# Talking-heads attention and squared-ReLU feed-forward on one core: one load of values at another step, and the score bursts of a batch's last block at other gathers

## Chip, cores and metric

The kernel runs on one core of one Trainium2 chip. The metric is device time in microseconds (us). The kernel before takes 598.79 us, the median of three runs (598.04 to 600.64).

## What is computed

Eight batches of attention with 12 heads, 448 positions and a head dimension of 64. The scores of the heads are mixed by a 12 x 12 matrix before the softmax, the probabilities by a second one behind it. The result, 3584 rows of 768, goes through a feed-forward layer with a squared ReLU and 2048 hidden units.

```python
scores = scale * np.matmul(q, k.transpose(0, 1, 3, 2))
scores = np.einsum('bhij,hg->bgij', scores, w_pre)
scores = scores - np.max(scores, axis=-1, keepdims=True)
attn = np.exp(scores)
attn = attn / (np.sum(attn, axis=-1, keepdims=True) + 1e-09)
attn = np.einsum('bhij,hg->bgij', attn, w_post)
attn_out = np.matmul(attn, v)
...
x = np.ascontiguousarray(attn_out.transpose(0, 2, 1, 3)).reshape(B * S, H * D)
h = np.maximum(x @ w_in, 0.0)
return (h * h @ w_out).astype(np.float32)
```

Inputs and output are float32; inside, the operands of matmuls are bfloat16.

## The kernel before

**Tiles and steps.** The queries of a batch are worked on ten at a time: ten queries by 12 heads are the 120 partitions of one tile. A batch has 45 such tiles (`NT`), and the eight batches make 360 steps, numbered through (`i`): batch 0 has steps 0 to 44, batch 1 has 45 to 89. One step does `mix` of tile i (matmul with the mixing matrix into `m_ps`, L420; exp on ScalarE, L424; every second tile the reciprocal of the sums on VectorE, L431, and the scaled mixing matrix `pn` on GpSimd, L434) and `unmix` of tile i - 4 (matmuls into `at_ps`, L449 and L453; copy into `at` by VectorE, L455). In the first 20 tiles of batch 0 scores and mixing are one set of matmuls (L406).

**Scores and gathers.** The scores are made for blocks of 128 queries, all heads: a batch from the second on has four blocks, which begin at queries 0, 128, 256 and 384 (`STARTS`); the last has 64 queries. A block's scores lie in a tile `S` with queries on the partitions, of which there are two in turn, so a block overwrites the one before the last. `score_burst` makes them for some pairs of heads: six matmuls (L359; twelve small ones, L365, for a last block) into six of the eight PSUM banks, and six copies into `S`, three by ScalarE (L369) and three by VectorE (L371). `gather` reshapes: one DMA on SP's queue (L388; two in a last block, L391) takes a tile's ten queries of all heads out of `S` into a tile `G` with 120 partitions, of which there are twelve. Gathers run ten steps ahead of their use (`AHEAD`). `FIRST` holds the tile at which the gathers of each block begin: 0, 13, 26 and 39. The scores of the following block are started at the gathers that `BURSTS` lists, counted from the block's first as 0: for the four blocks at [5, 8], [5, 8], [6] and [0, 3]. So the scores of the next batch's first block are made at the gathers of tiles 39 and 42, which stand at steps 29 and 32 of each batch (74 and 77 for batch 1). Tile 38 is the last to read the block that their `S` tile held before.

**Loads.** GpSimd issues all loads from DRAM, each at the top of a given step (`at_load`), in one queue (q0), with a cast to bfloat16. A batch's values come in three loads (`load_v`): the first rows of each group for the lower 64 partitions (L252), those for the upper 64 (L252), and the seventh row for the lower partitions (L248, the third load). There are two tiles of values, for even and odd batches. The values are first used in the matmuls of `av_unit` (L227 for the first three slots, L234 for the last two), three steps after a third of the tiles has been unmixed; for batch 1 this is step 66. `V1_AT` holds the steps at which the three loads of batch 1 are issued; `KQ_AT`, `W1_AT` and `W2_AT` those of keys and queries of batches 1 and 2 and of the weights. Later batches load their values at steps 34, 37 and 40 of the batch before.

**Feed-forward.** The hidden units of a batch (`ffn1_unit`, matmuls L278, relu on ScalarE L284, square on GpSimd or VectorE L289) and the output (`ffn2_unit`, matmuls L322, copy by VectorE L331, stores on SP L303) fill the steps of the next batch, spread by `fill`.

**Order.** The order on TensorE and GpSimd is the program's own (`manual_schedule`); VectorE's and ScalarE's instructions are put in order by a scheduler; SP's gathers and stores stand in one queue.

Of the kernel before, what the change touches and what calls it, by code (L numbers as in the profile page):

```python
# [30 lines left out]
STARTS = {0: (FQ, S - 128)}  # L31
FIRST = {0: (FUSED, 32)}
BURSTS = {0: ([4, 8], [5, 8])}
for _b in range(1, B):
    STARTS[_b], FIRST[_b], BURSTS[_b] = (0, 128, 256, 384), (0, 13, 26, 39), ([5, 8], [5, 8], [6], [0, 3])
GATHERS_AT = 2
HALF = H // 2
TT = 15
# [5 lines left out]
KQ_AT = {1: (4, 7, 10, 12), 2: (49, 51, 53, 55)}  # L44
W1_AT = (-1, 1, 3, 14, 16, 18)
W2_AT = (27, 29, 31, 33, 36, 39, 42, 45)
V1_AT = (46, 48, 56)
EARLY = ((21, 0, 0, 2), (29, 0, 2, 4), (38, 1, 0, 4), (52, 2, 0, 4))
FFN2_AT = 60
MAIN = 3 * 128  # L50
# [3 lines left out]
def kernel(  # L54
# [422 lines left out]
    with tc.manual_schedule(engines={PE, POOL}):  # L477
# [12 lines left out]
        def at_load(i, f, *args):  # L490
            loads.setdefault(i, []).append(lambda: f(*args))

        at_load(6, load_v, 0, 2)
        for x in range(3):
            at_load(V1_AT[x], load_v, 1, x)
        for x in range(4):
# [108 lines left out]
```

## Time and profile before

| | us |
|---|---|
| median of three runs | 598.79 |
| the profiled execution | 596.65 |
| its span, first to last instruction | 594.9 |
| VectorE busy in it | 401.7 |
| ScalarE busy | 380.7 |
| GpSimd busy | 355.5 |
| SP's stretch of 14 gather issues of batch 1's last block, from 120.86 us on | 11.68 |

The profile is that of one execution. PE is TensorE's matmuls, PEld its weight loads, DVE is VectorE, ACT ScalarE, POOL GpSimd, SP the queue of gathers and stores. A row of instructions in order of time reads: start, length, engine, line, operation, output<-input, shape, count, and in brackets the engine's idle time before it with what ended it. A row of waits reads: who waited, for whom, total us, times, longest. The clock row has a digit for each of 40 equal slices of the span, in tenths of full speed.

### The profile page before, as it was taken

The page shows a single profiled execution, that of the slowest core. Times are in us where ns is not written, and L with a number is a line of the kernel's source. Part 1 is how long each engine was busy: PE and PEld are TensorE (multiplying, and loading weights), DVE is VectorE, ACT ScalarE, POOL GpSimd, SP SyncE. Part 2 cuts the span into 40 slices and gives each one's busy share as a digit, 9 for nine tenths or more (in the row PEclk, how much of TensorE's full clock was granted, in tenths as well). Part 3 has the DMA queues.
Part 4 walks back from the last instruction along what each step waited for, and adds up shares of the span by engine and source line. Part 5 has one row for each costly group of instructions (what it writes and reads, how often), then busy time and mean ns, then how long its engine had stood idle before and what let it go on. Part 6 is the DMA issues. An engine that isn't in the chain of part 4 may idle for free.

```text
span 594.9 us, 18505 instructions
## 1 busy us (share of the span) xinstructions
PE 568.8 (96%) x6735; PEld 364.4 (61%) x6735; DVE 401.7 (68%) x995; ACT 380.7 (64%) x1114; POOL 355.5 (60%) x812
## 2 busy tenths in 40 slices
PE   4999999798999999999999999999999999999997
PEld 2577776464665665666665665655665666666554
DVE  7758759486877668777877668867777667655011
ACT  3747977476877548775777548775678548762410
POOL 6467896264579436784479436783486535772740
PEclk9999999898999999999999999999999999999999
DMA  9998999389557955688557955687643865432113
GB/s 129 156 192 171 184 196 178 74 130 200 135 106 121 167 118 99 122 132 160 116 81 130 173 122 102 116 134 144 125 81 65 126 136 110 87 50 54 28 26 81
DMA packets 85579, 72.28 MB, mean 122 GB/s; under 512 B 18768, under 2 KB 80496, under 8 KB 85488
## 3 DMA queue, kind: packets, MB, share of 16 engines
q1 hardware_dynamic: 49354, 47.30, 36.1%
q0 software_dynamic: 35552, 23.60, 30.2%
q8 instruction: 53, 0.87, 0.6%
q10 hardware_dynamic: 582, 0.21, 0.1%
q14 instruction: 38, 0.31, 0.1%
HBM read 47.28 MB, written 11.01 MB: 98 GB/s over the span
## 4 chain that ended last, share of the span: by engine, by line
PE 86%; DMA 7%; ACT 2%; POOL 2%; issue 1%; DVE 1%; SPq 0%; ACTq 0%; POOLq 0%; DVEq 0%
PE o_ps L322 23%; PE h_ps L278 23%; PE m_ps L420 10%; PE at_ps L449 9%; PE ot_ps L227 5%; PE s_ps L359 4%; PE m_ps L406 4%; DMA G<-S 3%; DMA v<-in_v_dram 2%; PE tr_ps L212 2%; PE ot_ps L234 2%; PE at_ps L453 2%; ACT e L424 1%; PE s_ps L365 1%; ACT S L369 1%
## 5 line engine op out<-in xcount | busy, mean ns | idle before, releaser
L455 DVE CAST at<-at_ps 128x480 bf16<-128x480 f32 (+1 forms) x360 | 206.7, 592 | 70.8 <-PE at_ps L453 53.7
L424 ACT ACTIVATE e<-m_ps 120x448 bf16<-120x448 f32 x360 | 196.2, 550 | 89.9 <-PE m_ps L420 49.0
L434 POOL TENSOR_SCALAR pn<-post,rc 120x120 bf16<-120x120 bf16 (+1 forms) x340 | 122.7, 371 | 175.8 <-DVE rc L431 111.7
L278 PE MATMUL h_ps<-xt,w 128*128 128x448 bf16 (+2 forms) x960 | 169.0, 315 | 2.3 <-ACT S L369 1.6
L322 PE MATMUL o_ps<-w,h 128*128 128x384 bf16 x768 | 140.5, 329 | 0.4
L420 PE MATMUL m_ps<-G,pre 120*120 120x448 bf16 (+1 forms) x340 | 122.0, 359 | 1.0 <-ACT S L369 0.5
L278 PEld LDWEIGHTS <-w 128*128 128x128 bf16 x960 | 84.3, 98 | 59.0 <-issue 8.7
L449 PE MATMUL at_ps<-pn,e 120*128 120x120 bf16 x1080 | 116.2, 216 | 4.0 <-ACT S L369 1.8
L289 POOL TENSOR_TENSOR h<-hr 128x384 bf16<-128x384 f32 (+1 forms) x144 | 105.7, 736 | 21.7 <-ACT hr L284 19.7
L449 PEld LDWEIGHTS <-e 120*128 120x128 bf16 x1080 | 85.8, 98 | 47.5 <-ACT S L369 4.5
L284 ACT ACTIVATE hr<-h_ps 128x448 f32<-128x448 f32 (+2 forms) x160 | 75.7, 478 | 46.8 <-PE h_ps L278 36.3
L322 PEld LDWEIGHTS <-h 128*128 128x128 bf16 x768 | 73.8, 99 | 47.2 <-issue 5.1
L369 ACT CAST S<-s_ps 128x448 bf16<-128x448 f32 x177 | 82.2, 551 | 14.4 <-PE s_ps L359 9.3
L371 DVE CAST S<-s_ps 128x448 bf16<-128x448 f32 x141 | 80.2, 614 | 3.8 <-DMA G<-S 3.5
L424 ACT ACTIVATION_READ_ACCUMULATOR e<-m_ps 120x1 f32 x360 | 75.5, 210 | 0.0
L331 DVE COPY osb<-o_ps 128x384 f32<-128x384 f32 x54 | 30.1, 557 | 58.7 <-PE o_ps L322 58.6
L431 DVE RECIPROCAL rc<-sm 120x1 f32<-120x1 f32 (+1 forms) x192 | 31.1, 162 | 43.7 <-ACT e L424 30.5
L420 PEld LDWEIGHTS <-pre 120*120 120x120 bf16 (+1 forms) x340 | 45.2, 133 | 20.8 <-issue 12.0
L240 ACT CAST xt<-ot_ps 128x450 bf16<-128x450 f32 (+1 forms) x48 | 25.4, 532 | 29.8 <-PE ot_ps L234 29.5
L437 POOL TENSOR_TENSOR en<-e,rc 120x128 bf16<-120x128 bf16 (+1 forms) x112 | 42.6, 380 | 0.0
L227 PE MATMUL ot_ps<-at,v 128*64 128x150 bf16 x864 | 42.2, 231 | 0.0
L359 PE MATMUL s_ps<-kT,qT 64*128 64x448 bf16 x276 | 39.6, 355 | 1.4 <-ACT hr L284 0.5
(62 smaller groups left out, 476.5 us busy)
## 6 DMA issues: line engine op xcount, KB each, us to landing
G<-S SPq DMA_DIRECT2D x276, 105.0 KB
out_dram<-osb SPq DMA_DIRECT2D x54, 192.0 KB
kst<-in_k_dram POOLq DMA_DIRECT2D x14, 336.0 KB, 5.8
qst<-in_q_dram POOLq DMA_DIRECT2D x14, 336.0 KB, 6.2
G<-S SPq DMA_DIRECT2D x70, 52.5 KB
v<-in_v_dram POOLq DMA_DIRECT2D x8, 384.0 KB, 9.0
w<-in_moe_w_in_dram POOLq DMA_DIRECT2D x6, 512.0 KB, 10.8
w<-in_moe_w_out_dram POOLq DMA_DIRECT2D x8, 384.0 KB, 8.2
```

The source lines that it names most:

```text
L227: nc.tensor.matmul(ps[64 * hh:64 * hh + 64, TQ * y:TQ * y + TQ], lhsT=vts[b % 2][:, g, r, :], rhs=at[:, r, g, :, :].rearrange("p t i -> p ...
L278: nc.tensor.matmul(ps[:, 0:n], lhsT=w1[ft // 8][:, c2, ft % 8 * 128:ft % 8 * 128 + 128], rhs=xts[b][:, c2, n0:n1], start=(c2 == 0), stop=( ...
L284: nc.scalar.activation(out=hr[:, 0:n], in_=ps[:, 0:n], func=ACT.Relu)
L289: eng.tensor_tensor(out=dst[:, x - o:y - o], in0=hr[:, x - n0:y - n0], in1=hr[:, x - n0:y - n0], op=ALU.mult)
L322: nc.tensor.matmul(ps[:, 0:384], lhsT=lhsT, rhs=w2[ft // 4][:, ft % 4, nt * 384:(nt + 1) * 384], start=(ft == 0), stop=(ft == FT - 1))
L369: nc.scalar.copy(out=sb[:, h, :], in_=ps[:, 0:S])
L371: nc.vector.tensor_copy(out=sb[:, h, :], in_=ps[:, 0:S])
L420: nc.tensor.matmul(ps[0:n, 0:S], lhsT=m[0:n, 0:n], rhs=Gs.pop(s)[0:n, :], start=True, stop=True)
L424: nc.scalar.activation(out=e[0:n, x, :], in_=ps[0:n, 0:S], func=ACT.Exp, scale=SCALE, accum_out=sm[0:n, x:x + 1])
L434: nc.gpsimd.tensor_scalar(out=esb[(b, t - z)][1][0:rows, :], in0=(post_gi if fused else post)[0:rows, :], scalar1=rc[0:rows, z:z + 1], sca ...
L449: nc.tensor.matmul(ps[:, RG * r:RG * r + RG], lhsT=e[0:n, tl % 2, P * r:P * r + P], rhs=pn[0:n, :], start=True, stop=True)
L455: nc.vector.tensor_copy(out=ats[(b, third)][:, 0:k, :, tl, :], in_=ps[:, 0:k * RG].rearrange("p (r g i) -> p r g i", r=k, i=IQ))
```

## The change

Two constants. The third load of batch 1's values is issued at the top of step 24, in place of step 56. The scores for a next batch's first block are started at the gathers 2 and 4 of a last block (its third and fifth, tiles 41 and 43), in place of 0 and 3; in step numbers these stand at 31 and 33 of a batch in place of 29 and 32. This holds for the six batches 1 to 6.

```diff
-    ..., BURSTS[_b] = (0, 128, 256, 384), (0, 13, 26, 39), ([5, 8], [5, 8], [6], [0, 3])
+    ..., BURSTS[_b] = (0, 128, 256, 384), (0, 13, 26, 39), ([5, 8], [5, 8], [6], [2, 4])
...
-V1_AT = (46, 48, 56)
+V1_AT = (46, 48, 24)
```

In the program's order TensorE's burst matmuls move, six at a time; the six copies behind each move with them on ScalarE and VectorE; GpSimd's issue of the load moves; SP's order is the same.

More of the change, by code (lines that the diff above doesn't have):

```diff
@@ L34 @@
 for _b in range(1, B):
-    STARTS[_b], FIRST[_b], BURSTS[_b] = (0, 128, 256, 384), (0, 13, 26, 39), ([5, 8], [5, 8], [6], [0, 3])
+    STARTS[_b], FIRST[_b], BURSTS[_b] = (0, 128, 256, 384), (0, 13, 26, 39), ([5, 8], [5, 8], [6], [2, 4])
 GATHERS_AT = 2
```

## The prediction

> **What bounds the kernel now.** I read the page first (busy shares, granted clock), then the list of waits, then the instructions in order of time around each long wait of TensorE.
>
> ```profile
> PE 568.8 (96%) x6735; PEld 364.4 (61%) x6735; DVE 401.7 (68%) x995; ACT 380.7 (64%) x1114; POOL 355.5 (60%) x812
> PEclk9999999898999999999999999999999999999999
> ...
> q0 software_dynamic: 35552, 23.60, 30.2%
> ```
>
> TensorE is busy for 568.8 of 594.9 us, so all that a change of order can win is in the 26 us left. Two slices of the clock row (about 104 to 119 and 134 to 149 us) stand under full speed; q0 is the queue of POOL's loads. The list of waits says who makes TensorE wait, and who waits for a DMA:
>
> ```profile
> PEld L234 <- DMA v<-in_v_dram: 3.6, 1, 3.6
> DVE S L371 <- DMA G<-S: 3.5, 5, 1.7
> PE ot_ps L234 <- DMA v<-in_v_dram: 3.4, 1, 3.4
> ACT S L369 <- DMA G<-S: 3.3, 2, 1.9
> ```
>
> There is one wait of 3.4 us for a load of values, and there are seven waits of the score copies (L369, L371) for a gather. In order of time, TensorE's matmuls:
>
> ```profile
> 101.98 1.47 PE L322 MATMUL o_ps<-w,h 128*128 128x384 bf16 x8
> ...
> 103.92 0.39 PE L227 MATMUL ot_ps<-at,v 128*64 128x150 bf16 x6
> 107.70 0.26 PE L234 MATMUL ot_ps<-at,v 128*64 128x80 bf16 x4 [3.39 <-DMA v<-in_v_dram]
> ...
> 110.59 2.10 PE L322 MATMUL o_ps<-w,h 128*128 128x384 bf16 x8
> ...
> 139.03 0.38 PE L449 MATMUL at_ps<-pn,e 120*128 120x120 bf16 x3 [1.78 <-ACT S L369]
> ...
> 389.66 1.29 PE L278 MATMUL h_ps<-xt,w 128*128 128x448 bf16 x6 [1.40 <-ACT S L369]
> ```
>
> These three are the only waits of TensorE over 0.9 us after the start. Stretches of time show what the others did in the first wait, and the clock after the first two (length; busy us of PE, PEld, DVE, ACT, POOL; clock; DMA share, GB/s):
>
> ```profile
> 104.00:107.70 3.70, 0.31 (x8) 0.13 (x8) 0.65 (x3) 0.89 (x4) 1.63 (x5) 1.00 0.72 172
> 108.46:111.88 3.42, 3.42 (x43) 2.44 (x37) 0.66 (x1) 1.70 (x4) 0.00 (x0) 0.50 0.00 0
> 139.18:142.60 3.42, 3.37 (x16) 1.85 (x15) 1.75 (x4) 2.16 (x7) 0.84 (x3) 0.50 1.26 233
> ```
>
> In the 3.70 us no engine is busy even for half the time: nothing else was late, and the load alone set the end. Then TensorE ran 3.42 us at half its clock.
>
> **Part one: the third load of batch 1's values from step 56 to step 24.** It removes nothing and adds nothing; one DMA issue of POOL moves forward.
>
> ```profile
> 49.36 0.70 POOL L434 TENSOR_SCALAR pn<-post,rc 120x120 bf16<-120x120 bf16 x2 [2.46 <-PE tr_ps L212]
> ...
> 92.81 0.80 POOL L248 DMA_DIRECT2D v<-in_v_dram  x1
> ```
>
> Issued at 92.81, the data were there when the wait ended, just under 107.70: some 14.8 us. It is the last of seven loads that POOL issues from 79.4 us on, so it arrives last. At step 24 (about 47 us) it has 57 us until the same use, and the earlier copy of this load for batch 0, also in a crowded stretch, took 14.1 us. So:
> - The wait at 107.70 goes: -3.39 us. Bounds -3.39 and 0 (something else late in its place: a rival below).
> - The half clock behind it goes: TensorE is busy for 3.42 of 3.42 us at 0.50, and the same work takes 1.71 at full clock: -1.71. The eight L322 matmuls show it, 2.10 us there (partly at full clock again) and 1.47 before. Bounds -1.71 and 0.
> - The issue takes 0.80 us of POOL at its new place. POOL sits idle for 2.46 us before 49.36, which is where its order puts the load, so 0. Without that cover pn would be 0.8 us late, and TensorE's at_ps (L449) waits for pn: +0.8 at most.
> - Queue q0: the loads issued behind it (eight of w_out, 52.9 to 77.6 us) move back. The load is 96 KB; at the 174 and 163 GB/s of the stretches 46.9-52.9 and 52.9-59.2 us that is 0.6 us. They land 6.3 to 8.7 us after issue, so the last by 86.4 us, and their first use (L322) is at 98.9: 12 us of cover, so 0. Gathers share those engines and could be 0.6 us late; they run ten steps ahead: 0, at most +0.6.
> - At step 56 POOL gains 0.80 us, ahead of an idle time of 2.90 us: 0.
>
> [...]
>
> **Part two: score bursts at the third and fifth gather of a batch's last block.** Six places (batches 1 to 6). The first burst of six matmuls moves two steps later, the second one step; the count of matmuls, copies and gathers is the same, and SP's order too. The first burst writes the S buffer of block two, whose last reader is the gather just before: its copies wait for that gather, keep six of eight PSUM banks, and TensorE stands. Seen at batch 5:
>
> ```profile
> 387.19 0.74 PE L359 MATMUL s_ps<-kT,qT 64*128 64x448 bf16 x6
> ...
> 389.07 1.40 ACT L369 CAST S<-s_ps 128x448 bf16<-128x448 f32 x3 [1.37 <-DMA G<-S]
> ```
>
> Two steps are some 3.3 us (594.9 / 360 = 1.65 each), more than the 1.9 us from the burst to its copies' start, so this wait goes: -1.40. At the other five places the same burst costs TensorE under 0.5 us each. All waits of copies for gathers sum to 6.8 us; 3.6 of these (1.9 and 1.7) belong to the stall at 139.03, which is a burst at the sixth gather of batch 2, not moved. That leaves 3.2 as the most that can be won; I take the row, 1.40.
>
> What it may cost: the bursts stand two steps apart, not three. DVE's three copies end 2.54 us after their burst began:
>
> ```profile
> 325.24 0.74 PE L359 MATMUL s_ps<-kT,qT 64*128 64x448 bf16 x6
> ...
> 326.10 1.68 DVE L371 CAST S<-s_ps 128x448 bf16<-128x448 f32 x3
> ```
>
> Against 3.3 us that leaves 0.8; at the shortest pair seen (122.17 to 125.81, three steps in 3.64, so two in 2.43) it is 0.1 short. Bounds 0 and six times 1.68 = 10.1; nearest are the rows, so +0.3 in all. Behind the second burst, SP's first gather of the next block comes two steps later: 3.3 against 2.54, no wait; if there were one, later gathers and the stores queue behind it, with ten steps (16 us) of cover.
>
> The stall at 139.03 I leave as it is: SP issues its gathers back to back there, and neither part touches that. [...]
>
> **Sum:** -3.39 - 1.71 - 1.40 + 0.3 = -6.2 us. The profiled execution took 596.65 us (span 594.9, 1.75 around it); less 6.2 that is 590.45. It lies 2.1 under the median of the timed runs (598.79; 598.04 to 600.64), and I take the difference from the median: 592.6 us.
>
> **Rivals.**
> 1. The load's wait is replaced by one for gathers. For: in the 3.7 us stall the DMAs moved 172 GB/s, 636 KB, six gathers of 105 KB: a backlog was cleared in the pause. Against: at that rate a gather takes 0.6 us and TensorE uses one per 1.65, with twelve buffers. If 3.39 comes back and the clock stays up: 598.79 - 1.71 - 1.1 = 596.0.
> 2. Part two wins nothing, or its closer bursts eat it: -5.1 with 0 to 2 back: 593.7 to 595.7.
> 3. Slower: with two steps between bursts the second finds its banks held at all six places, and each stall is like that at 139.03: 6 x 1.78 = 10.7, so 598.79 - 6.5 + 10.7 = 603.0. It decides from 1.6 us a place ((6.5 + 3.0) / 6). For: 139.03 shows what six held banks do. Against: there the copies waited for a gather; here for nothing but their engines.
> [...]
> 5. The stall at 139.03 goes as well, being fed by a queue that now starts from another state: 592.6 - 1.78 - 1.71 = 589.1.
> 6. The load at step 24 does not arrive earlier: nothing supports this, as its order on POOL is fixed; under 0.01.
>
> **Numbers.** Forecast 0.50; rivals 1: 0.12, 2: 0.14, 3: 0.06, 4: 0.08, 5: 0.10. A measurement of this kernel tells from no change what exceeds 0.5% (3.0 us). Faster than 595.8: forecast, 4, 5 and nearly all of 2: 0.80. Same: rival 1 and what is left of 2: 0.14. Slower: 0.06. The range runs from rival 5 with a little more from part two (588) to rival 1 with the delays of part one (597).
>
> **What would show it.** Right: no L234 wait for v near 104 us and no stretch at 0.50 behind it; the L252 and L248 loads in a new order; no DMA wait of S copies at the first burst (the 1.40 near 389, now some 5 us earlier). Wrong: a wait for G at L420 from step 66 on; TensorE waiting for S copies right after a second burst; pn late near 49 us.

## The result, and the profile after

The changed kernel takes 590.06 us, the median of six runs (588.0 to 592.45); the kernel before, in six runs, 598.04 (597.13 to 600.64). The ratio is 0.9861, with a 95% interval of 0.9829 to 0.9894: some 8 us faster, where 6.2 were forecast. Ratios, and the sums over many runs below, leave out those runs of a kernel that lie more than 1.5% above its fastest (602.26 and 603.27 us of the kernel before, 602.14 and 602.86 of the one with the load at step 60), while the medians count every run. The profiled executions differ by 6.4 us (596.65 and 590.27; spans 594.9 and 588.5).

From the page of the changed kernel, busy shares and granted clock:

```profile
PE 566.3 (96%) x6735; PEld 363.4 (62%) x6735; DVE 401.5 (68%) x995; ACT 380.4 (65%) x1114; POOL 355.2 (60%) x812
...
PEclk9999999998999999999999999999999999999999
```

TensorE runs the same 6735 matmuls and is busy for 566.3 us in place of 568.8; one slice of the clock is under full speed where there were two. From its list of waits:

```profile
DVE S L371 <- DMA G<-S: 2.0, 2, 1.6
...
ACT S L369 <- DMA G<-S: 1.8, 1, 1.8
```

No wait for v is left, and of seven waits of score copies for a gather three remain. TensorE's matmuls in order of time:

```profile
104.02 0.39 PE L227 MATMUL ot_ps<-at,v 128*64 128x150 bf16 x6
104.24 0.24 PE L234 MATMUL ot_ps<-at,v 128*64 128x80 bf16 x4
...
106.17 1.47 PE L322 MATMUL o_ps<-w,h 128*128 128x384 bf16 x8
...
134.00 0.33 PE L449 MATMUL at_ps<-pn,e 120*128 120x120 bf16 x3 [1.68 <-ACT S L369]
...
134.83 2.73 PE L322 MATMUL o_ps<-w,h 128*128 128x384 bf16 x8
...
384.11 0.74 PE L359 MATMUL s_ps<-kT,qT 64*128 64x448 bf16 x6
384.85 1.29 PE L278 MATMUL h_ps<-xt,w 128*128 128x448 bf16 x6
```

The L234 matmuls start 0.22 us after the L227 ones (3.78 before). The eight L322 matmuls behind them take 1.47 us (2.10 before). In batch 5 the matmuls after the first burst follow at once, where TensorE had stood for 1.40 us. Stretches of time (columns as before):

```profile
104.00:107.70 3.70, 3.70 (x77) 2.94 (x76) 1.41 (x4) 2.67 (x8) 1.74 (x5) 1.00 0.61 172
...
134.85:138.27 3.42, 3.42 (x17) 1.74 (x16) 1.57 (x4) 1.71 (x6) 1.07 (x3) 0.50 1.26 236
```

In the 3.70 us in which TensorE did 0.31 us of work it is now busy throughout, and DMA moves as much as before (172 GB/s): no other wait came in place of the load's. The third stall, near 139 us before, is still there near 134, 1.68 us long, and still with a half clock behind it.

The length of each batch, from the exp (L424) of its first tile to that of the next batch's, worked out from the traces, shows where the time came from. The two kernels with one part of the change are the first experiments below. Each row is one execution; a stretch of 3.42 us at a clock of 0.50, as above, adds some 1.71 (an estimate: half of it) to the batch in which it falls.

| us | batch 0 | 1 | 2 | 3 | 4 | 5 | 6 |
|---|---|---|---|---|---|---|---|
| before | 59.54 | 69.95 | 66.03 | 64.82 | 69.85 | 66.23 | 70.56 |
| changed | 60.07 | 64.66 | 65.90 | 64.89 | 70.02 | 64.83 | 70.51 |
| load alone | 59.84 | 64.44 | 65.94 | 66.23 | 69.88 | 65.66 | 70.91 |
| bursts alone | 59.91 | 65.75 | 66.58 | 64.90 | 70.02 | 64.83 | 70.07 |

Batch 1 gave 5.29 us, batch 5 gave 1.40, and batch 0 lost 0.53.

### The profile page after: what moved, and what is told of

It is laid out like the page before. It is cut to its first block, busy times and chain, and to the rows that moved or that the text cites. A ratio compares the mean times of both kernels' runs of the same rounds, so it can differ in the third digit from the quotient of the medians.

```text
span 588.5 us, 18497 instructions
## 1 busy us (share of the span) xinstructions
PE 566.3 (96%) x6735; PEld 363.4 (62%) x6735; DVE 401.5 (68%) x995; ACT 380.4 (65%) x1114; POOL 355.2 (60%) x812
## 4 chain that ended last, share of the span: by engine, by line
PE 88%; ACT 4%; DVE 3%; DMA 2%; POOL 1%; issue 1%; ACTq 0%; POOLq 0%; DVEq 0%; SPq 0%
PE o_ps L322 25%; PE h_ps L278 24%; PE m_ps L420 11%; PE at_ps L449 10%; PE ot_ps L227 5%; PE s_ps L359 4%; PE m_ps L406 4%; ACT e L424 2%; PE tr_ps L212 2%; PE ot_ps L234 2%; ACT S L369 2%; PE at_ps L453 2%; DMA G<-S 1%; PE s_ps L365 1%; DVE w L195 1%
## 5 line engine op out<-in xcount | busy, mean ns | idle before, releaser
L424 ACT ACTIVATE e<-m_ps 120x448 bf16<-120x448 f32 x360 | 196.3, 551 | 87.7 <-PE m_ps L420 48.4
L322 PE MATMUL o_ps<-w,h 128*128 128x384 bf16 x768 | 140.0, 328 | 0.4 <-ACT e L424 0.2
L420 PE MATMUL m_ps<-G,pre 120*120 120x448 bf16 (+1 forms) x340 | 121.7, 359 | 2.0 <-ACT S L369 1.4
L449 PE MATMUL at_ps<-pn,e 120*128 120x120 bf16 x1080 | 116.2, 216 | 3.6 <-ACT S L369 1.7
L289 POOL TENSOR_TENSOR h<-hr 128x384 bf16<-128x384 f32 (+1 forms) x144 | 105.7, 736 | 20.9 <-ACT hr L284 19.1
L449 PEld LDWEIGHTS <-e 120*128 120x128 bf16 x1080 | 85.7, 98 | 47.3 <-ACT S L369 4.6
L322 PEld LDWEIGHTS <-h 128*128 128x128 bf16 x768 | 73.4, 98 | 48.5 <-issue 5.7
L424 ACT ACTIVATION_READ_ACCUMULATOR e<-m_ps 120x1 f32 x360 | 75.6, 210 | 0.0
L420 PEld LDWEIGHTS <-pre 120*120 120x120 bf16 (+1 forms) x340 | 45.2, 133 | 20.2 <-issue 11.9
L227 PE MATMUL ot_ps<-at,v 128*64 128x150 bf16 x864 | 41.6, 229 | 0.0
```

Of the source, the lines that this page charges most:

```text
L227: nc.tensor.matmul(ps[64 * hh:64 * hh + 64, TQ * y:TQ * y + TQ], lhsT=vts[b % 2][:, g, r, :], rhs=at[:, r, g, :, :].rearrange("p t i -> p ...
L289: eng.tensor_tensor(out=dst[:, x - o:y - o], in0=hr[:, x - n0:y - n0], in1=hr[:, x - n0:y - n0], op=ALU.mult)
L322: nc.tensor.matmul(ps[:, 0:384], lhsT=lhsT, rhs=w2[ft // 4][:, ft % 4, nt * 384:(nt + 1) * 384], start=(ft == 0), stop=(ft == FT - 1))
L420: nc.tensor.matmul(ps[0:n, 0:S], lhsT=m[0:n, 0:n], rhs=Gs.pop(s)[0:n, :], start=True, stop=True)
L424: nc.scalar.activation(out=e[0:n, x, :], in_=ps[0:n, 0:S], func=ACT.Exp, scale=SCALE, accum_out=sm[0:n, x:x + 1])
L449: nc.tensor.matmul(ps[:, RG * r:RG * r + RG], lhsT=e[0:n, tl % 2, P * r:P * r + P], rhs=pn[0:n, :], start=True, stop=True)
```

## The experiments

All ratios are to the kernel before, run beside them, and only they can be compared: its median there was 598.8 us (beside the two single parts, the load at step 49 and the bursts one step apart), 597.28 (beside the last three kernels) and 596.34 (beside the others).

**One part alone.** The first undoes the bursts:

```diff
-    ... ([5, 8], [5, 8], [6], [2, 4])
+    ... ([5, 8], [5, 8], [6], [0, 3])
```

> The load at step 24 alone, bursts as before. Theory (the load's wait and the half clock behind it are 5.1 us of the gain, the bursts some 1.1 more): 5.1 us under before less up to 0.6 for the load's place on POOL, ratio 0.991 to 0.993; no wait of L234 near 104 us; the wait of 1.4 us near 389 us is still there, some 5 us earlier. Rival (the gain is the bursts'): ratio 0.997 or more. Rival (a wait for gathers takes the load's place): a wait at L420 between 104 and 112 us.

Measured: 592.77 us, ratio 0.9909 (0.9872 to 0.9945), as the theory had it. No wait for v; TensorE's waits behind first bursts are back, in two batches (matmuls in order of time, as in the fences below where nothing else is said):

```profile
249.64 1.29 PE L278 MATMUL h_ps<-xt,w 128*128 128x448 bf16 x6 [1.33 <-ACT S L369]
...
384.95 1.29 PE L278 MATMUL h_ps<-xt,w 128*128 128x448 bf16 x6 [0.87 <-ACT S L369]
```

The first is in batch 3, where the profile of before had none: which batch pays for its first burst, and how much, changes from one execution to the next, so the one row of 1.40 us was a sample of it. Counting those over 0.4 us, the profiles with the bursts as before have 1.40 us of such waits (the kernel before), 2.20 (this run), 1.34 (the load at step 49) and 1.81 (the load at step 60). At L420 there is no wait over 0.4 us between 104 and 112 us: the gathers did not take the load's place.

The second undoes the load:

```diff
-V1_AT = (46, 48, 24)
+V1_AT = (46, 48, 56)
```

> The bursts at the third and fifth gather alone, the load at step 56 as before. Theory: the 3.4 us wait for v near 107 us and the stretch at half clock behind it stay; the first bursts' copies no longer wait for a gather; 0 to 2 us under before, ratio 0.9965 to 1.000. Rival (the bursts' closer distance costs TensorE): ratio over 1.002, with TensorE waiting for S copies behind second bursts.

Measured: 595.14 us, ratio 0.9954 (0.9917 to 0.9991), a little under the stretch that was expected. The two parts alone give 0.9% and 0.5%, together 1.4%, which is what the change gives: they add, as far as intervals of 0.4% to either side can tell. The wait for v is there, and no wait behind a first burst over 0.9 us in any of the six batches. But in this execution the wait was shorter, 2.41 us, and the clock did not halve behind it (1.00 from 107.0 to 113.8 us):

```profile
106.99 0.26 PE L234 MATMUL ot_ps<-at,v 128*64 128x80 bf16 x4 [2.41 <-DMA v<-in_v_dram]
...
108.94 1.47 PE L322 MATMUL o_ps<-w,h 128*128 128x384 bf16 x8
```

The eight L322 matmuls take 1.47 us here, not 2.10. The half clock is no fixed companion of this wait. In this profile no stretch before the last matmul is at half clock (1.000 in the mean), so batch 1 is 4.20 us shorter than in the kernel before although its load is issued at the same step: 0.98 of that is the shorter wait, 3.4 the two missing stretches. One profile's batch lengths do not price a part; the ratios do.

**Why the load was late.** Is it the loads ahead of it in the queue? The load at step 49, just ahead of the loads of keys and queries, with bursts as before:

```diff
-V1_AT = (46, 48, 56)
+V1_AT = (46, 48, 49)
```

> The load at step 49, just ahead of the four loads of keys and queries, bursts as before. Theory (the load came late because it stood last in a queue that works in order, not because it was issued too late as such): it lands near 96 us, 8 us before its use, and the time is as with the load at step 24 alone, ratio 0.991 to 0.993; keys and queries land up to 1 us later, without a wait. Rival (a load issued this late cannot land in time): a wait of 1 us or more at L234 stays.

Measured: 592.33 us, ratio 0.990 (0.9847 to 0.9953), as with step 24. GpSimd issues it at 84.64 us, ahead of the first load of keys (instructions of GpSimd in order of time):

```profile
84.64 0.79 POOL L248 DMA_DIRECT2D v<-in_v_dram  x1
85.42 0.66 POOL L87 DMA_DIRECT2D kst<-in_k_dram  x1
```

TensorE's matmuls at the use of the values:

```profile
105.49 0.39 PE L227 MATMUL ot_ps<-at,v 128*64 128x150 bf16 x6
105.71 0.24 PE L234 MATMUL ot_ps<-at,v 128*64 128x80 bf16 x4
```

It landed 11.6 us after its issue, at 96.2. Seven steps earlier and ahead of four large loads were enough; step 24 was not needed. The edit changes both the place and the time of issue (8.2 us earlier), and no run parts them. But the landings in the traces follow the order of issue: in the kernel before the six loads ahead land at 89.16, 93.44, 96.58, 99.51, 102.18 and 104.98 us and this one, small as it is, at 107.65; here it lands between the values (94.87) and the keys issued 0.78 us after it (98.43), and the last load of queries lands at 106.61, so behind that one it would have missed its use at 105.7.

The other way, four steps later still:

```diff
-V1_AT = (46, 48, 56)
+V1_AT = (46, 48, 60)
```

> The kernel before with the load at step 60, four steps later still. Theory (the wait is the landing time less the time of use): the load is issued some 6 us later; as the queue ahead of it is then nearly empty, it lands 3 to 6 us later, the wait is 6 to 9 us and the clock halves behind it in every run: ratio 1.005 to 1.015. Rival (the use is late for another reason and the load only looks like the releaser): ratio 1.000 to 1.003.

Measured: 598.57 us, ratio 0.9996 (0.9954 to 1.0038): missed. The load was issued 8.5 us later than at step 56 but landed only 2.7 us later, 9.0 us after its issue in place of 14.8: of the six loads ahead three had landed by then, and a fourth did 0.5 us later, where in the kernel before one had:

```profile
110.37 0.34 PE L234 MATMUL ot_ps<-at,v 128*64 128x80 bf16 x4 [5.14 <-DMA v<-in_v_dram]
```

The wait is 5.14 us, 1.75 more than before, and the clock halved at its end here: six L227 matmuls take 0.57 us behind it and 0.39 ahead of it. Batch 1 is only 0.41 us longer than before (70.36), as no half clock followed its later stall. In the timed runs nothing of that can be told from the noise: the ratio is also what the rival expected, and the theory's larger wait shows in the profile alone.

**The bursts' distance.** One step between them, not two:

```diff
-    ... ([5, 8], [5, 8], [6], [2, 4])
+    ... ([5, 8], [5, 8], [6], [3, 4])
```

> The load at step 24, the bursts one step apart (fourth and fifth gather). Theory (copies end 2.5 us after their burst began, so one step of some 1.65 us is too short): TensorE waits 0.5 to 1.2 us for S copies at each of the six places, 3 to 7 us over the changed kernel: ratio to before 0.991 to 0.998. Rival (banks never held TensorE, only the wait for a gather did): as the changed kernel, 0.986.

Measured: 590.7 us, ratio 0.988 (0.982 to 0.994). The theory falls by the profile, which has no wait of TensorE over 0.4 us behind a second burst. In batch 5 the second burst begins 2.36 us after the first, and TensorE goes on:

```profile
384.23 0.78 PE L359 MATMUL s_ps<-kT,qT 64*128 64x448 bf16 x6
384.94 1.31 PE L278 MATMUL h_ps<-xt,w 128*128 128x448 bf16 x6
...
386.59 0.74 PE L359 MATMUL s_ps<-kT,qT 64*128 64x448 bf16 x6
387.49 0.35 PE L420 MATMUL m_ps<-G,pre 120*120 120x448 bf16 x1 [0.16 <-ACT e L424]
```

In this profile a burst's copies hold TensorE once for 0.9 us, at L449 as in the stall that stayed, and elsewhere for 0.2 us at most; ScalarE's copies wait for a gather once, for 1.1 us. A small cost is not excluded: batches 4 and 6 are 0.48 and 0.72 us longer here than in the changed kernel, without such a wait.

**The load's place on GpSimd.** Step 22 in place of 24:

```diff
-V1_AT = (46, 48, 24)
+V1_AT = (46, 48, 22)
```

> The changed kernel with the load at step 22. Theory (at step 24 its issue stands behind pn and en of the pair of tiles 22 and 23 and puts off those of 24 and 25 by 0.8 us, which costs batch 0 some 0.5 us; at step 22 it falls into POOL's idle time): batch 0 is 0.3 to 0.6 us shorter in the profile, the rest the same; too small for the ratio (0.985 to 0.987). Rival (the 0.5 us is chance): batch 0 as long as in the changed kernel.

Measured: 590.61 us, ratio 0.9885 (0.9836 to 0.9935); batch 0 is 60.55 us long. The theory falls: batch 0 is no shorter, and it is also 59.91 us with the load at step 56 and 60.54 with it at step 60. The 0.53 us of the changed kernel's batch 0 lie within what this batch varies, and nothing is shown of a cost at step 24.

**The stall that stayed.** It is a burst at the sixth gather of batch 2 whose copies wait for the gather of batch 1's tile 44. Two gathers later, in every batch from the second on:

```diff
-    ... ([5, 8], [5, 8], [6], [2, 4])
+    ... ([7, 10], [5, 8], [6], [2, 4])
```

> The changed kernel, and the scores of a batch's second block started at gathers 7 and 10 of its first block in place of 5 and 8. Theory (the wait of 1.7 us near 134 us is six banks held by copies that wait for the gather of tile 44, so two gathers more of distance end it): no wait of TensorE over 0.9 us is left after the start, batch 1 is 1.5 to 3.5 us shorter with the half clock that follows the wait, ratio to before 0.980 to 0.984. Rival (SP's queue is late there as such): the wait moves to an L420 that waits for G, or to the next burst, ratio 0.985 to 0.987.

Measured: 589.78 us, ratio 0.9873 (0.9831 to 0.9915). In the profile the stall is gone, and batch 1 is 59.91 us long (64.66). But batch 2 is 67.59 (65.90), with a wait for a gather:

```profile
141.10 0.40 PE L420 MATMUL m_ps<-G,pre 120*120 120x448 bf16 x1 [0.95 <-DMA G<-S]
```

The stall went as the theory had it, but the rival's sign, a wait for a gather at L420, came in its place, and the ratio is not the 0.980 to 0.984 of the theory; the timed runs cannot be told from the changed kernel's.

Fewer loads beside that gather: the values of batch 2 at steps 88, 91 and 94 in place of 79, 82 and 85.

```diff
-                    at_load(NT * b + 34 + 3 * x, load_v, b + 1, x)
+                    at_load(NT * b + (43 if b == 1 else 34) + 3 * x, load_v, b + 1, x)
```

> The changed kernel, with the three loads of batch 2's values nine steps later (steps 88, 91 and 94). Theory (the gather of tile 44 lands late, 6.4 us after its issue, because loads share the DMA engines with it): fewer loads in that stretch, the gather lands 1 to 2 us sooner and the wait near 134 us falls from 1.7 to under 0.8 us; ratio 0.982 to 0.986. Rival (SP's own issue time, 14 issues back to back in 11.7 us, sets it): the wait stays at 1.4 to 1.8 us, ratio 0.986.

Measured: 593.36 us, ratio 0.9922 (0.9887 to 0.9957), where 0.982 to 0.986 was expected and the changed kernel has 0.9861. The wait fell to 0.47 us, where the nine profiles with these loads and this burst in their old places have 0.94 to 2.50; so the loads beside the gather were at least part of its cause. But the next burst now waits for a gather, while the moved loads are under way (one of them lands at 149.03 us):

```profile
132.99 0.33 PE L449 MATMUL at_ps<-pn,e 120*128 120x120 bf16 x3 [0.47 <-ACT S L369]
...
151.33 0.48 PE L449 MATMUL at_ps<-pn,e 120*128 120x120 bf16 x3 [3.95 <-ACT S L369]
```

So they were moved forward, to steps 67, 70 and 73:

```diff
-                    at_load(NT * b + 34 + 3 * x, load_v, b + 1, x)
+                    at_load(NT * b + (22 if b == 1 else 34) + 3 * x, load_v, b + 1, x)
```

> The changed kernel, with the three loads of batch 2's values twelve steps earlier (steps 67, 70 and 73), where the DMA engines are half idle. Theory (loads that share the DMA engines make the gather of tile 44 late, and later places only move the collision to the next burst, as at steps 88 to 94): the wait near 134 us falls to 0.6 us or less and no new one over 1 us appears; batch 1 is 2 to 3.5 us shorter; the share of runs with a half clock after it falls; ratio to before 0.981 to 0.986, 1 to 3 us under the changed kernel run beside it. Rival (the earlier loads delay gathers of steps 68 to 75): a wait at L420 or L212 between 108 and 122 us, no gain.

Measured: 588.93 us, ratio 0.9867 (0.9827 to 0.9906). The two waits that are left of it:

```profile
134.53 0.33 PE L449 MATMUL at_ps<-pn,e 120*128 120x120 bf16 x3 [0.21 <-ACT S L369]
...
149.45 0.33 PE L449 MATMUL at_ps<-pn,e 120*128 120x120 bf16 x3 [0.63 <-ACT S L369]
```

Batch 1 is 61.63 us long, 3.03 less than in the changed kernel; 1.71 of that is a half clock which did not follow here (mean granted clock 0.998). The ratio missed its expected stretch by a little, and its profiled execution lost part of the gain elsewhere (batch 0, which the edit does not touch, is 61.25 us, batch 2 66.55). With the bursts at the fourth and fifth gather besides (the edit shown above):

> As the run with early loads of batch 2's values, and the bursts at the fourth and fifth gather. Theory (one step between bursts costs nothing, as seen; the first burst one step later still gains distance from the gather it waits for): equal to the run with early loads, within 1 us. Rival (closer bursts do cost where the loads no longer hide it): 1 to 3 us longer than that run.

Measured: 589.81 us, ratio 0.9872 (0.9834 to 0.9911): equal, as the theory had it. The changed kernel, beside the two and without an edit:

> The changed kernel itself, beside the other two on the same chip: ratio to before 0.984 to 0.990 by the earlier runs; the mean granted clock of its runs is nearer to 1 than that of the kernel before (by some 0.004), and each run at half clock once is about 1.7 us longer than one without.

Measured: 590.97 us, ratio 0.989 (0.9849 to 0.9931), or 6.6 us, where the first six runs gave 8. Its mean granted clock is 0.9975 against 0.9948 of the kernel before, 0.0027 more where 0.004 was expected; what one half clock adds to a run cannot be told from six runs. The kernel with early loads has the lowest median of all, 2.0 us under this, but the intervals overlap: whether it beats the changed kernel stays open.

**The clock over all runs.** Each run has its span and mean granted clock; (1 - clock) x span is an estimate of what the clock took. The table sums over the runs of before that stood beside the experiments (51) and those of the changed kernel (12).

| us | mean time | taken by the clock | the rest |
|---|---|---|---|
| before, 51 runs | 597.5 | 3.3 | 594.2 |
| changed, 12 runs | 590.4 | 1.2 | 589.2 |
| difference | -7.1 | -2.1 | -5.0 |

The 2.1 us are known to 0.8 either way, by the spread of the runs. Part of the 3.3 and the 1.2 costs nothing: in the 13 profiles 0.0 to 1.2 us of it (0.5 in the mean) falls behind the last matmul. Over the 51 runs of before, a run's time rises by 1.04 us for each us that the clock took (correlation 0.83). The 13 with a clock of 0.991 or less have a mean of 600.2 us, the 9 with 0.999 or more 594.5.

## Why the prediction was right

- **The load alone set the end near 107 us (-3.39 us).** Right: moved to step 24 or 49 the wait goes, nothing comes in its place, and batch 1 shrinks. A single execution's 3.39 is one draw: the same wait was 2.41 us with the bursts alone.
- **The half clock behind it (-1.71 us).** Right that it goes, mis-sized as a mean. I charged one half-clock stretch in every run of before and let all others cancel between the kernels. Over the runs the clock took 3.3 us before and 1.2 after: 2.1 us won. That wait is not always followed by a half clock, and other waits of before are. That one certain half clock came so near to this is partly luck. Together with the wait, the load was put at 5.1 us; alone it gave 5.4 (3.3 to 7.6).
- **First bursts (-1.40 us, at most 3.2).** Right in mechanism: all waits behind first bursts over 0.9 us are gone wherever the bursts are moved. In the profile batch 5 gives exactly 1.40. The four profiles with the bursts as before have 1.34 to 2.20, so the row taken was at the lower end. With the 0.3 for closer bursts this part was put at 1.1 us; alone it gave 2.7 (0.5 to 5.0), a size the runs don't fix. Waits together were put at -3.39 - 1.40 + 0.3 = -4.5; the runs show -5.0.
- **Closer bursts (+0.3 us, rival 3 up to +10.7).** The bound was much too wide: even at one step of distance no wait of TensorE over 0.4 us behind a second burst shows. The stall at 139.03, from which I priced rival 3, comes of copies that wait for a gather, and such a wait is what the change removes here.
- **The load's issue falls into POOL's idle 2.46 us.** Wrong in place: it stands behind the pn and en that follow that idle time.

```profile
49.09 0.70 POOL L434 TENSOR_SCALAR pn<-post,rc 120x120 bf16<-120x120 bf16 x2 [2.46 <-PE tr_ps L212]
...
50.10 0.83 POOL L248 DMA_DIRECT2D v<-in_v_dram  x1
50.97 0.70 POOL L434 TENSOR_SCALAR pn<-post,rc 120x120 bf16<-120x120 bf16 x2
```

  The pn of the next tiles came 0.54 us later than in the profile of before (50.43), inside the bound of 0.8; step 22 gave no shorter batch 0, so it cost nothing that could be shown. The last of the w_out loads behind it landed at 86.54 us (85.83 before), far ahead of its use, as the prediction had it.
- **The stall at 139.03 stays.** Right: 1.68 us in the changed kernel, so rival 5 falls. Its cause, given as SP's back-to-back issues, was at best half told: with those issues as they were and the loads moved away, it falls to 0.47 or 0.21 us. A half clock followed it in four of the nine profiles that have it.
- **Rival 1** (gathers late instead) falls with the 3.70 us of full TensorE work at 104 us. **Rival 2** falls with the bursts alone at 0.9954, though its interval ends at 0.9991. **Rival 4**, by which only the wait would count, falls with the table of the clock (2.1 us won there). In these executions the clock halved behind waits of 1.68 and 1.78 us (0.50 over 3.42 us each) and stayed up behind 2.41 (1.00).
- **The median against the profile.** I set the sum against the median of before; three runs more brought that from 598.79 to 598.04. Against the gains of the two sets of runs (8 and 6.6 us) the forecast of 6.2 is a little small, in the bursts and the clock.

## What to carry to other kernels

Look for the load that stands last in a queue and not only for one issued late: here the small load behind six large ones landed 2.67 us after the last of them, and four places forward were enough. Copies that wait for a DMA to finish reading their target keep their PSUM banks and stop TensorE, for 1.40 and 1.78 us here; put distance between the last reader and the next writer, and move a load away from the transfer they wait for only after looking at which burst it will meet next. Take a stall's price over several runs with their clock, not from one profile.

## What was not expected

The clock's part in the spread. The time of one and the same kernel went from 592.71 to 601.8 us in the 51 runs of the table, and much of that follows the mean granted clock (correlation 0.83 above). The three stretches at half clock ahead of the last matmul in the profiles of the two kernels are 3.42 us long each (108.46 to 111.88 and 139.18 to 142.60 us before, 134.85 to 138.27 changed). Around the end of the wait of 3.95 us, in the run with later loads, the clock is 0.73 over the 3.93 us ahead of that end and 0.50 over the 4.67 us behind it.

Whether a half clock follows a wait is not told by the wait's length: it was seen at the end of waits of 1.68, 1.78, 3.39, 3.95 and 5.14 us, not behind 2.41. What decides it is not shown here.
